# A gated linear-attention kernel with a low-rank mixer: six PSUM banks become one tile, read two or more banks at a time

## The chip, the cores and the metric

The kernel runs on one core of a Trainium2 chip. The core has TensorE (matrix products; PE for the products, PEld for the weight loads in the profile), VectorE (DVE), ScalarE (ACT), GpSimd (POOL) and SyncE (SP, which here only issues transfers). TensorE writes its results into PSUM, which has eight banks of 512 fp32 values in each of 128 partitions; VectorE and ScalarE read them there. The metric is the device time of one launch in microseconds (us), lower is better; a time is the median of several runs. Everything is fp32.

## What is computed

Two blocks follow each other. The first is a recurrence over 768 positions for 4 batches and 8 heads of 48 values, with a complex gate for each position and channel; the second mixes its result over positions with a rank-32 product and over channels with a two-layer network.

```python
scale = np.minimum(mag, 0.999) / (mag + 1e-06)      # mag = |a_re + i a_im|
a_re_n, a_im_n = (a_re * scale, a_im * scale)
for t in range(S):
    new_re = ar * S_re - ai * S_im
    new_im = ar * S_im + ai * S_re
    kv = np.einsum('bhd,bhe->bhde', k[:, :, t], v[:, :, t])
    S_re, S_im = (new_re + kv, new_im)
    y[:, :, t] = np.einsum('bhd,bhde->bhe', q[:, :, t], S_re)
...
h = x.transpose(0, 2, 1) @ U @ V                    # x: (4, 768, 384), from y
u = x + h.transpose(0, 2, 1)
return u + np.maximum(u @ w_ch1, 0.0) @ w_ch2       # w_ch1: 384 x 1536
```

## The kernel before

The 24 pieces of 128 positions (6 for each batch) are called chunks, and each is cut into two halves of 64 positions. For a chunk the gates are turned into logarithms and phases and summed over the positions by products with a triangular matrix (L744, L748 and L808 to L814), and become factors `es`, `cs`. `prep` multiplies q and k by them (L459) into `qkc`, turns each of q and k by 16 small transposes into two PSUM banks, one for each half (L869), and ScalarE copies each bank to `QK` (L875). `chain` then makes the products inside the halves (L898, masked into `AT` by VectorE, L901), the state of each half (L918; VectorE adds it to the running state `GM` and `G` through the helper `bounded`, L465), and the output of the chunk in two banks `y`: first `inside` (L948), AT times v, then `before` (L956), q times the state that went in, first for half 0 and then for half 1, accumulated onto it. ScalarE copies the two banks to `xo` (L965, L967).

`mixer` works on pairs of chunks (12 pairs, `m`). It makes the rank sums (L991), spreads them back over four banks (L1014) which VectorE adds to `xo` one bank at a time (`mixed`, L1019), turns `xo` into two banks (L1033) which VectorE and ScalarE copy to `uT`, one each (L1038), and then makes the two layers: `up` (L1052) for the first pairs and `up_fewer` (L1159), a scheme with fewer products whose sums are collected in `h` by ScalarE (L1167) and VectorE (L462, L1171), for the others; then `down` (L1248) and `down_two` (L1291), whose sums VectorE adds to `xo` before the transfer out (L1235).

Six of the eight PSUM banks are shared by all of this: six tiles `BANKS[0..5]` of 128 x 512, handed round in turn to every result that is not `up`, `down`, or (for most pairs) two of the five sums of `up_fewer`. Those use two banks of their own (`psM`), in which the results are called `up`, `down`, `few` and so on in the profile; what lies in the six is called `bank`. Waits between engines are not written by hand: the framework follows, tile by tile, what each instruction reads and writes and sets semaphores from it.

The order of work on every engine is written out: each helper (`PE`, `ACT`, `DVE`, `POOL`, `SP`) records an operation (a group of instructions) in `plan`, and at the end `plan.order()` emits them in the sequence of the list `ORDER`, 2190 numbers long. On each engine the instructions keep that order. `SPARE` puts some products of the identity ahead of early operations (`idle`, L1441 and L1445); their results are not used.

## Time and profile before

| | us |
|---|---|
| median of 3 runs | 540.3 (540.25 to 540.9) |
| the profiled execution | 539.81 |
| its span (first to last instruction) | 537.9 |
| TensorE products busy | 514.1 |
| TensorE weight loads busy | 468.5 |
| VectorE busy | 421.6 |
| ScalarE busy | 294.8 |
| mean granted TensorE clock | 0.995 of full |

A row of instruction groups names the line, the engine, the operation, output<-inputs, the shapes and the count; then the group's busy time, the mean duration of one in ns, and the idle time of its engine just before it, with what ended that. In a timeline the two leading numbers are the start and the length in us. A row of a table by stage has the stretch, its length, and for each engine its busy time and number of instructions, then the granted clock, the share of the DMA engines and GB/s. Products are pipelined, so that the end of one is modelled and consecutive ones overlap: the pitch of a group, from its start to the start of the next, is its cost on TensorE.

### The profile page before, as it was taken

The page shows a single profiled execution, that of the slowest core. Times are in us where ns is not written, and L with a number is a line of the kernel's source. Part 1 is how long each engine was busy: PE and PEld are TensorE (multiplying, and loading weights), DVE is VectorE, ACT ScalarE, POOL GpSimd, SP SyncE. Part 2 cuts the span into 40 slices and gives each one's busy share as a digit, 9 for nine tenths or more (in the row PEclk, how much of TensorE's full clock was granted, in tenths as well). Part 3 has the DMA queues.
Part 4 walks back from the last instruction along what each step waited for, and adds up shares of the span by engine and source line. Part 5 has one row for each costly group of instructions (what it writes and reads, how often), then busy time and mean ns, then how long its engine had stood idle before and what let it go on. Part 6 is the DMA issues. An engine that isn't in the chain of part 4 may idle for free.

```text
span 537.9 us, 17099 instructions
## 1 busy us (share of the span) xinstructions
PE 514.1 (96%) x7482; PEld 468.5 (87%) x7482; DVE 421.6 (78%) x837; ACT 294.8 (55%) x528; POOL 31.8 (6%) x61
## 2 busy tenths in 40 slices
PE   2789999899999999999999999999999999999996
PEld 1677786757999999999999999999999999999996
DVE  8788988999999998797997797797788364746352
ACT  5879998884786876456746746444544412011100
POOL 1000000000020000100200000100010000000010
PEclk9989999999999999999999999999999999999999
DMA  9948987642337142412450620500141000000011
GB/s 225 193 85 202 196 147 192 199 67 46 61 91 128 31 84 46 87 41 46 87 110 24 108 44 14 109 1 16 18 96 41 4 9 16 9 16 1 1 46 34
DMA packets 150689, 39.94 MB, mean 74 GB/s; under 512 B 145912, under 2 KB 147408, under 8 KB 150608
## 3 DMA queue, kind: packets, MB, share of 16 engines
q1 hardware_dynamic: 148400, 34.43, 32.7%
q0 software_dynamic: 2208, 4.35, 2.4%
q8 instruction: 60, 0.98, 0.8%
q14 instruction: 21, 0.17, 0.1%
HBM read 33.60 MB, written 4.76 MB: 71 GB/s over the span
## 4 chain that ended last, share of the span: by engine, by line
PE 81%; DVE 8%; ACT 7%; DMA 2%; issue 1%; SPq 0%; DVEq 0%; ACTq 0%
PE down L1291 29%; PE few L1159 13%; PE bank L1159 12%; PE bank L898 4%; PE bank L869 4%; PE bank L956 3%; PE bank L918 3%; PE bank L948 2%; PE up L1052 2%; PE bank L1014 1%; PE bank L808 1%; ACT gate L456 1%; DMA stage<-in_moe_w_ch_dram 1%; ACT cs L456 1%; PE bank L744 1%
## 5 line engine op out<-in xcount | busy, mean ns | idle before, releaser
L1291 PE MATMUL down<-w,h 128*128 128x192 f32 x396 | 73.1, 331 | 0.0
L875 ACT COPY QK<-bank 112x512 f32<-112x512 f32 x96 | 51.9, 593 | 26.3 <-PE bank L869 24.5
L1291 PEld LDWEIGHTS down<-w,h 128*128 128x128 f32 x396 | 64.3, 190 | 1.4
L462 DVE TENSOR_TENSOR xo<-down,xo 128x192 f32<-128x192 f32 (+1 forms) x79 | 30.1, 387 | 22.6 <-PE down L1291 22.3
L1167 ACT COPY h<-bank 128x512 f32<-128x512 f32 x25 | 14.3, 587 | 58.1 <-PE bank L1159 58.1
L456 ACT ACTIVATE gate<-gate 128x768 f32<-128x768 f32 (+1 forms) x50 | 39.8, 797 | 9.7 <-DVE wide L716 5.9
L459 DVE TENSOR_TENSOR QKC<-qk,cs 128x768 f32<-128x768 f32 x48 | 44.9, 952 | 0.1
L1291 PE MATMUL down<-stage 128*128 128x192 f32 x198 | 37.5, 330 | 0.0
L1052 PE MATMUL up<-uT,w 128*128 128x256 f32 x144 | 34.2, 387 | 2.0 <-ACT h L456 0.9
L1167 ACT COPY h<-few 128x512 f32<-128x512 f32 x35 | 20.4, 588 | 23.4 <-PE few L1159 23.4
L1291 PEld LDWEIGHTS down<-stage 128*128 128x128 f32 x198 | 32.4, 190 | 0.7
L1052 PEld LDWEIGHTS up<-uT,w 128*128 128x128 f32 x144 | 26.4, 190 | 7.2 <-ACT extra L456 1.5
L462 DVE TENSOR_TENSOR h<-bank,h 128x512 f32<-128x512 f32 x16 | 11.0, 690 | 27.3 <-PE bank L1159 16.8
L453 ACT ACT_TABLE_LOAD x24 | 30.8, 1283 | 1.1 <-PEq L1497 0.7
L869 PE MATMUL bank<-ident,QKC 64*112 64x64 f32 x768 | 29.2, 222 | 1.7 <-DVE GM L929 1.3
L869 PEld LDWEIGHTS bank<-ident,QKC 64*112 64x112 f32 x768 | 24.5, 132 | 7.2 <-issue 2.0
L794 POOL DMA_DIRECT2D gate<-F x15 | 12.0, 798 | 317.4 <-DVE F L817 177.6
L1159 PE MATMUL bank<-extra,w 128*128 128x128 f32 x232 | 30.1, 276 | 0.1
L1235 POOL DMA_DIRECT2D out_dram<-xo x32 | 19.7, 683 | 166.6 <-DVE xo L462 126.7
L1159 PEld LDWEIGHTS bank<-extra,w 128*128 128x128 f32 x232 | 28.2, 192 | 0.4 <-DVE AT L901 0.3
L456 ACT ACTIVATE cs<-F 128x384 f32<-128x384 f32 x48 | 23.8, 518 | 8.3 <-DVE F L817 7.1
L456 ACT ACTIVATE es<-bank 128x384 f32<-128x384 f32 x48 | 20.2, 497 | 14.6 <-PE bank L744 13.5
(185 smaller groups left out, 1179.0 us busy)
## 6 DMA issues: line engine op xcount, KB each, us to landing
stage<-in_moe_w_ch_dram SPq DMA_DIRECT2D x12, 768.0 KB
gate<-in_a_re_dram SPq DMA_DIRECT2D x24, 192.0 KB
gate<-in_a_im_dram SPq DMA_DIRECT2D x24, 192.0 KB
qk<-in_q_dram SPq DMA_DIRECT2D x24, 192.0 KB
qk<-in_k_dram SPq DMA_DIRECT2D x24, 192.0 KB
VP<-in_v_dram SPq DMA_DIRECT2D x24, 192.0 KB
out_dram<-xo POOLq DMA_DIRECT2D x12, 192.0 KB, 2.5
out_dram<-xo POOLq DMA_DIRECT2D x20, 96.0 KB, 2.4
```

What stands on the lines that cost most here:

```text
L453: ACT(1.4, rank, lambda: nc.scalar.preload_act_table_set(name), writes=[TABLE])
L456: return nc.scalar.activation(out=o, in_=i, func=f, **kw)
L459: nc.vector.tensor_tensor(out=o, in0=a, in1=b, op=OP.mult)
L462: nc.vector.tensor_tensor(out=o, in0=a, in1=b, op=OP.add)
L869: nc.tensor.transpose(out=get(*ps[r])[0:DQ, h], in_=get(*qkc)[at, h].rearrange("p u d -> p (u d)")[:, 0:DQ], identity=ident[at, at], tile_ ...
L875: nc.scalar.copy(out=get(*QK)[:, u].rearrange("p (h t) -> p h t", t=CH)[:, :, r * HC:(r + 1) * HC], in_=get(*ps[r])[0:DQ])
L898: nc.tensor.matmul(out=get(*ps0)[r:r + HC, h], lhsT=k_of(h, r, HC), rhs=q_of(h, r, HC), start=True, stop=True, tile_position=(0, r))
L1052: nc.tensor.matmul(out=get(*ps)[:, e], lhsT=w1[:, f, (ff + e) * 128:(ff + e + 1) * 128], rhs=get(*uT)[:, f], start=(f == 0), stop=(f == KD ...
L1159: nc.tensor.matmul(out=get(*ps)[:, q], lhsT=w()[:, q * 128:(q + 1) * 128], rhs=v[0](), start=(n == 0 and q == 0), stop=True, skip_group_ch ...
L1167: ACT(c_act(n3 * CH) - 0.045, RU, lambda i=i, k=k: nc.scalar.copy(out=at(i, k), in_=get(*ps)), [ps], [o])
L1235: queue.dma_start(out=out[b, c * CH:(c + 1) * CH, lo:hi], in_=get("xo", i)[:, lo:hi])
L1291: nc.tensor.matmul(out=get(*to)[:, part], lhsT=x(j), rhs=y[:, j], start=(first and j == 0), stop=(j == KH - 1), skip_group_check=not first)
```

## The change

The six bank tiles become one tile `BANKS` of 128 x 6 x 512; `bank_of` notes which bank a result has, and `beside` merges results that lie in neighbouring banks into one access. With it:

- `prep`: ScalarE copies both halves of a turned q or k by one instruction where the two banks are neighbours (40 of 48), by two where they are bank 5 and bank 0.
- `mixed`: VectorE adds the spread sums of up to four banks by one instruction: 19 instructions for 48.
- `turned`: for most pairs ScalarE alone copies both banks to `uT` (one instruction of 768 elements for each partition, or two of 384), where VectorE and ScalarE copied one each. VectorE has 9 copies fewer, ScalarE 2 more.
- `chain`: `before` (both halves) is recorded ahead of `inside`, and starts the accumulation; `inside` no longer names the states among what it reads.
- `ORDER` is another list, of 2097 numbers; one entry of `SPARE` moves with the numbering.

TensorE has the same 4233 matrix instructions. The number of neighbouring groups on TensorE with a different shape of its array (whole, halves of rows, halves of columns, quarters and so on) goes from 209 to 199. ScalarE's copies go from 245 to 207; VectorE's additions and multiplications of two tensors go from 497 to 468.

```diff
 SPARE = {
-    122: 2, 132: 10, 193: 14, 217: 5,
+    122: 2, 132: 10, 193: 14, 215: 5,
 }
...
@@ -378,9 +374,11 @@
     plan = Plan()
     makers, T, pools = {}, {}, {}
     banks = pool("banks", space=PSUM)
-    BANKS = [banks.tile([128, 512], FP, name="bank%d" % n) for n in range(6)]
-    for a in BANKS:
-        nc.vector.memset(a[HC // 2:HC], 0.0)
+    NB = 6
+    BANKS = banks.tile([128, NB, 512], FP, name="banks")
+    for n in range(NB):
+        nc.vector.memset(BANKS[HC // 2:HC, n], 0.0)
+    bank_of = {}
 
     def buffer(base, tag, bufs, shape, space=None, padded=None):
 
@@ -405,14 +403,25 @@
         if tag == "M":
             buffer(base, "psM", 2, shape, PSUM, padded)
             return
-        plan.buffer(base, "psS", len(BANKS), True)
+        plan.buffer(base, "psS", NB, True)
 
         def view():
-            a = BANKS[sum(plan.tag.get(b) == "psS" for b in T) % len(BANKS)]
+            bank_of[base] = sum(plan.tag.get(b) == "psS" for b in T) % NB
+            a = BANKS[:, bank_of[base]]
             size = padded or shape
             a = a[0:shape[0], 0:math.prod(size[1:])]
             return a[:, 0:shape[1]] if len(shape) == 2 else a.rearrange("p (x y) -> p x y", x=size[1])[:, 0:shape[1], 0:shape[2]]
         makers[base] = view
+
+    def beside(ps):
+
+        out = []
+        for n in range(len(ps)):
+            if n and bank_of[ps[n]] == bank_of[ps[n - 1]] + 1:
+                out[-1][1] = n + 1
+            else:
+                out.append([n, n + 1])
+        return [(lo, hi, BANKS[:, bank_of[ps[lo]]:bank_of[ps[lo]] + hi - lo]) for lo, hi in out]
 
 
     def c_act(n):
@@ -870,10 +879,11 @@
                                             identity=ident[at, at], tile_position=(r * HC, 0))
             PE(TURN, R1, turn, [qkc], ps, takes=[QK], way=5, steps=2 * H)
 
-            for r in range(2):
-                def keep(u=u, r=r, ps=ps):
-                    nc.scalar.copy(out=get(*QK)[:, u].rearrange("p (h t) -> p h t", t=CH)[:, :, r * HC:(r + 1) * HC], in_=get(*ps[r])[0:DQ])
-                ACT(c_act(HH * CH) - 0.06, R1, keep, [ps[r]], [QK + ((u, r),)])
+            def keep(u=u, ps=ps):
+                to = get(*QK)[:, u].rearrange("p (h r t) -> p r h t", r=2, t=HC)
+                for lo, hi, a in beside(ps):
+                    nc.scalar.copy(out=to[:, lo:hi], in_=a[0:DQ].rearrange("p r (h t) -> p r h t", t=HC))
+            ACT(c_act(2 * HH * CH) - 0.06, R1, keep, ps, [QK + (u,)])
 
 
 
@@ -946,7 +956,7 @@
                     for u in range(2):
                         h, at = 2 * p + u, slice(r * HC, (r + 1) * HC)
                         nc.tensor.matmul(out=get(*y[u])[side(r, u), p], lhsT=get(*ATi)[at, h], rhs=get(*VPi)[at, h],
-                                         start=(p == 0), stop=(c == 0 and r == 0), tile_position=(r * HC, (r ^ u) * HC),
+                                         start=(c == 0 and r == 0 and p == 0), stop=True, tile_position=(r * HC, (r ^ u) * HC),
                                          skip_group_check=True)
 
         def before(r):
@@ -954,12 +964,13 @@
                 for u in range(2):
                     h = 2 * p + u
                     nc.tensor.matmul(out=get(*y[u])[side(r, u), p], lhsT=q_of(h, r * HC, HC),
-                                     rhs=get(*(mid_G if r else ("G", i - 1)))[:, h], start=False, stop=True,
+                                     rhs=get(*(mid_G if r else ("G", i - 1)))[:, h], start=(p == 0), stop=False,
                                      tile_position=(0, (r ^ u) * HC), skip_group_check=True)
-        PE(0.44, RR, inside, [VPi, ATi, mid_G] + ([("G", i - 1)] if c else []), y, way=3, takes=[xi], steps=4 * H)
         if c:
             PE(0.467, RR, lambda: before(0), [QK, ("G", i - 1)], [y[0] + (0,), y[1] + (0,)], way=1, steps=2 * H)
         PE(0.467, RR, lambda: before(1), [QK, mid_G], [y[0] + (1,), y[1] + (1,)], way=1, steps=2 * H)
+        PE(0.44, RR, inside, [VPi, ATi], y, way=3, takes=[xi], steps=4 * H)
+
         def halves(a):
             return a.rearrange("p (a u d) -> p a u d", u=2, d=D)
         ACT(c_act(HH * D) + 0.02, RR, lambda: nc.scalar.copy(out=halves(get(*xi))[:, :, 0], in_=get(*y[0])), [y[0]], [xi + (0,)])
@@ -1016,31 +1027,41 @@
             PE(0.45, R0, products, [r, ("V", 0)] + [uT + ("kept",)] * (m >= AHEAD), ps, way=4, steps=4 * NP)
             return ps
 
-        def mixed(n, ps):
-            u = XO[i0 // MC % len(XO)].rearrange("p c (f n t) -> p n c f t", n=NP, t=R)[:, n]
-            DVE(c_dve(MC * RC), R0, lambda: add(u, get(*ps)[:, 0:MC].rearrange("p c (f t) -> p c f t", t=R), u), [ps],
-                [("xo", i0 + cc) for cc in range(MC)])
+        def mixed(ps):
+            u = XO[i0 // MC % len(XO)].rearrange("p c (f n t) -> p (c f) n t", n=NP, t=R)
+
+            def f():
+                for lo, hi, a in beside(ps):
+                    add(u[:, :, lo:hi], a[:, :, 0:MC * RC].rearrange("p n (f t) -> p f n t", t=R), u[:, :, lo:hi])
+            DVE(c_dve(MC * DM) + 0.1, R0, f, ps, [("xo", i0 + cc) for cc in range(MC)])
 
         def turned():
             us = [("xo", i0 + cc) for cc in range(MC)]
             tr = [out_of("uTp", ("pair", m, r), [128, MC * KD, HC], [128, H, HC]) for r in range(2)]
+            late = plan.tag[tr[0]] != "psS"
 
             def turn():
                 for cc in range(MC):
                     for f in range(KD):
                         for r in range(2):
                             at = slice(r * HC, (r + 1) * HC)
-                            nc.tensor.transpose(out=get(*tr[r])[:, cc * KD + f], in_=get(*us[cc])[at, f * 128:(f + 1) * 128],
+                            nc.tensor.transpose(out=get(*tr[r])[:, f * MC + cc], in_=get(*us[cc])[at, f * 128:(f + 1) * 128],
                                                 identity=ident[at, at], tile_position=(r * HC, 0))
             PE(0.39, R0, turn, us, tr, way=5, steps=2 * KD * MC)
-            for r in range(2):
-                def keep(copy, r=r):
-                    copy(out=get(*uT).rearrange("p f (c s t) -> p s c f t", c=MC, t=HC)[:, r],
-                         in_=get(*tr[r]).rearrange("p (c f) t -> p c f t", c=MC))
-                if r:
-                    ACT(c_act(MC * KD * HC) - 0.045, R0, lambda keep=keep: keep(nc.scalar.copy), [tr[r]], [uT + (r,)])
-                else:
-                    DVE(c_dve(MC * KD * HC), R0, lambda keep=keep: keep(nc.vector.tensor_copy), [tr[r]], [uT + (r,)])
+            def keep(copy, lo, hi, a):
+                copy(out=get(*uT).rearrange("p f (c s t) -> p (f c) s t", c=MC, t=HC)[:, :, lo:hi],
+                     in_=a[:, :, 0:MC * KD * HC].rearrange("p s (f t) -> p f s t", t=HC))
+
+            def both():
+                for x in beside(tr):
+                    keep(nc.scalar.copy, *x)
+            if ahead or late:
+                for r, (add_to, c, copy) in enumerate(((DVE, c_dve(MC * KD * HC), nc.vector.tensor_copy),
+                                                       (ACT, c_act(MC * KD * HC) - 0.045, nc.scalar.copy))):
+                    add_to(c, R0, lambda r=r, copy=copy: copy(
+                        out=get(*uT).rearrange("p f (c s t) -> p (f c) s t", c=MC, t=HC)[:, :, r], in_=get(*tr[r])), [tr[r]], [uT + (r,)])
+            else:
+                ACT(c_act(2 * MC * KD * HC) - 0.045, R0, both, tr, [uT + (0,)])
 
         def up(ff):
             ps = out_of("up", (m, ff), [128, 2, N], None)
@@ -1341,8 +1362,7 @@
                 ranked()
             for ff in range(0, NP, 2):
                 corrected(ff)
-        for n, ps in enumerate(spread()):
-            mixed(n, ps)
+        mixed(spread())
         if m >= AHEAD:
             turned()
         if m < AHEAD:
```

## Prediction

> **What bounds the kernel now.** I read the page first, then the table by stage, then who waited for whom.

> ```profile
> span 537.9 us, 17099 instructions
> ...
> PE 514.1 (96%) x7482; PEld 468.5 (87%) x7482; DVE 421.6 (78%) x837; ACT 294.8 (55%) x528; POOL 31.8 (6%) x61
> ...
> PE 81%; DVE 8%; ACT 7%; DMA 2%; issue 1%; SPq 0%; DVEq 0%; ACTq 0%
> ```
> ```profile
> 10.20:33.00 22.80, 17.91 (x248) 14.51 (x248) 19.26 (x33) 18.31 (x32) 0.00 (x0) 0.95 0.92 193
> 33.00:60.00 27.00, 26.66 (x456) 20.07 (x456) 23.61 (x41) 23.61 (x45) 0.00 (x0) 0.98 0.70 156
> 60.00:97.00 37.00, 35.82 (x737) 27.66 (x734) 32.04 (x57) 34.30 (x60) 0.95 (x1) 1.00 0.80 174
> 97.00:127.40 30.40, 28.14 (x123) 18.20 (x121) 28.49 (x46) 23.48 (x35) 1.52 (x2) 1.00 0.46 101
> 127.40:200.00 72.60, 72.48 (x1402) 67.23 (x1402) 69.85 (x130) 51.56 (x92) 5.24 (x8) 1.00 0.44 82
> 200.00:300.00 100.00, 100.00 (x1411) 95.47 (x1411) 83.81 (x172) 60.79 (x111) 9.25 (x14) 1.00 0.32 61
> ```
> ```profile
> PE bank L748 <- DVE GL L462: 10.2, 1, 10.2
> PE bank L918 <- ACT QK L875: 1.7, 1, 1.7
> ```

> From 127.4 us on TensorE is never idle; its stream of products alone sets the time. Ahead of that it is idle for 10.2 us at the start and then for 4.9 + 0.3 + 1.2 + 2.3 = 8.7 us (first column after the length against the length, first four rows). So the change can win little by faster copies: there is hardly a wait to take away. What it can lose is the overlap that keeps TensorE full, and that can be seen in one place:

> ```profile
> 391.44 1.11 PE L869 MATMUL bank<-ident,QKC 64*112 64x64 f32 x32
> ...
> 391.94 0.95 DVE L459 TENSOR_TENSOR QKC<-qk,cs 128x768 f32<-128x768 f32 x1
> 392.15 2.05 ACT L875 COPY QK<-bank 112x512 f32<-112x512 f32 x4 [0.93 <-PE bank L869]
> 392.48 0.81 PEld L918 LDWEIGHTS bank<-VP,QKC 64*48 64x48 f32 x64
> 392.48 0.94 PE L918 MATMUL bank<-VP,QKC 64*48 64x48 f32 x64
> ```

> ScalarE reads four turned banks from 392.15 to 394.20, and meanwhile TensorE writes the states into two others (392.48). Six tiles make this possible.

> **The change: one tile.** Waits come from what the framework notes for each tile. In both built programs I followed the wait values of the semaphores: for each access of TensorE, VectorE or ScalarE to one of the six banks, are the other engines' last accesses to any of the six, earlier in the program, known to be over? Before, in 3,011 of 7,608 such pairs; after, in all 7,457. One tile is treated as one thing: a product into bank 5 waits for the copy out of banks 3 and 4, and a ScalarE copy waits for a VectorE read of another bank. A typical pair of rows of the two programs:

> ```
> before: L1038 TensorCopy uT<-bank_65 128x2x3x64 [waits PE_49]
> after:  L1052 TensorCopy uT<-banks 128x768 [waits DVE_49,PE_49]
> ```

> So all work on the six banks is one chain through three engines, in the order of the program. Only TensorE's work on the two other banks (`down`, `up`, part of `few`) still runs beside reads, where it stands between them in the order. I price that gap by gap: a gap is a run of reads between two stretches of products into the six banks. The changed program has 184 gaps with 410 reads: 241 by ScalarE, 169 by VectorE. Their rows:

> ```profile
> L875 ACT COPY QK<-bank 112x512 f32<-112x512 f32 x96 | 51.9, 593 | 26.3 <-PE bank L869 24.5 <-DVE QKC L459 1.8
> L456 ACT ACTIVATE gate<-gate 128x768 f32<-128x768 f32 x43 | 36.2, 843 | 9.5 <-DVE wide L716 5.8 <-DMA gate<-in_a_im_dram 3.0
> ...
> L456 ACT ACTIVATE es<-bank 128x384 f32<-128x384 f32 x48 | 20.2, 497 | 14.6 <-PE bank L744 13.5 <-PE bank L748 1.0
> L967 ACT COPY xo<-bank 64x192 f32<-64x192 f32 x48 | 15.0, 314 | 11.7 <-PE bank L956 11.0
> ...
> L1167 ACT COPY h<-bank 128x512 f32<-128x512 f32 x25 | 14.3, 587 | 58.1 <-PE bank L1159 58.1
> L456 ACT ACTIVATE F<-bank,magic 128x384 f32<-128x384 f32 x24 | 13.9, 580 | 15.7 <-PE bank L808 14.7 <-PE bank L811 0.6 <-PE bank L814 0.3
> ...
> L1038 ACT COPY uT<-bank 128x384 f32<-128x384 f32 x10 | 4.8, 478 | 18.2 <-PE bank L1033 18.2
> ```
> ```profile
> L1171 DVE CUSTOM_DVE_ANT_1 h<-bank,h 128x512 f32<-128x512 f32 x32 | 21.6, 687 | 8.2 <-ACT h L1167 4.6 <-PE bank L1159 3.2
> L901 DVE COPY_PREDICATED AT<-mask,bank 128x512 f32<-128x512 int32 x24 | 17.6, 732 | 8.5 <-ACT xo L967 4.6 <-PE bank L898 3.6
> L462 DVE TENSOR_TENSOR xo<-bank,xo 128x192 f32<-128x192 f32 x48 | 15.3, 352 | 5.6 <-PE bank L1014 5.5
> L817 DVE SCALAR_TENSOR_TENSOR F<-F,bank 128x384 f32<-128x384 f32 x24 | 13.2, 549 | 6.7 <-ACT F L456 6.6
> ...
> L465 DVE CUSTOM_DVE_ANT_0 GM<-bank,G 112x384 f32<-112x384 f32 x20 | 11.1, 555 | 2.3 <-PE bank L918 1.5 <-ACT extra L456 0.2
> ...
> L462 DVE TENSOR_TENSOR h<-bank,h 128x512 f32<-128x512 f32 x16 | 11.0, 690 | 27.3 <-PE bank L1159 16.8 <-ACT h L1167 10.5
> ```

> The merged forms aren't in the trace. The 112x1024 copy costs at least what 768 elements cost (0.84 us) and at most two copies of 512 (1.19); the line through 0.314 (192) and 0.593 (512) gives 0.15 + 0.00087 n, so 1.03 us, near the middle, which I take (over 40 copies the bounds are 6 to 8 us apart from it). The merged sums lie on VectorE's line, 0.15 + 0.00105 n, between 0.35 and 0.95 us, and cannot cost more than the additions they replace.

> ScalarE: 40 x 1.03 + 16 x 0.593 + 48 x 0.497 + 24 x 0.58 + 25 x 0.587 + 72 x 0.315 (L965 as L967) + 7 x 0.82 + 5 x 0.478 + 1.2 for four small ones = 135 us. VectorE: 44 x 0.555 (GM, G) + 24 x 0.732 + 24 x 0.549 + 32 x 0.687 + 16 x 0.69 + 12.5 for the 19 merged sums (6 x 0.352 + 2 x 0.555 + 6 x 0.755 + 5 x 0.955) + 5 for ten others = 106 us. Together 241 us.

> Each gap also has its handing over, which these rows show:

> ```profile
> 452.32 1.06 PE L1159 MATMUL bank<-uT,gate 128*128 128x128 f32 x8
> ...
> 453.22 1.14 PE L1291 MATMUL down<-w,stage 128*128 128x192 f32 x6
> 453.42 0.69 DVE L1171 CUSTOM_DVE_ANT_1 h<-bank,h 128x512 f32<-128x512 f32 x1
> ```
> ```profile
> 98.75 0.59 ACT L456 ACTIVATE extra<-up 128x512 f32<-128x512 f32 x1
> ...
> 99.39 2.46 PEld L1052 LDWEIGHTS up<-uT,w 128*128 128x128 f32 x12 [1.24 <-ACT extra L456]
> ...
> 103.44 0.84 ACT L456 ACTIVATE gate<-gate 128x768 f32<-128x768 f32 x1
> ...
> 104.32 0.96 DVE L720 SCALAR_TENSOR_TENSOR GL<-gate,GL 128x768 f32<-128x768 f32 x1 [0.18 <-ACT gate L456]
> ```

> TensorE to reader 0.20 us (453.42 after its stream ended at 453.22), reader to TensorE 0.05 (99.34 to 99.39), reader to reader 0.04 (104.28 to 104.32). 184 x 0.25 + 65 changes of reader x 0.04 = 49 us. All gaps: 241 + 49 = 290 us.

> **What hides it.** From each gap I take TensorE's own work on the two other banks that stands in it, by pitches: 6 products of L1291 0.97 us (below), 8 of L1159 0.90 (452.32 to 453.22), and so on; what it has more than the gap is lost. Example: after a chunk's transposes (L869) come GM, the merged copy of q, G and two copies of k: 0.555 + 1.03 + 0.555 + 2 x 0.593 = 3.33, with handing over 3.70 us; two groups of L1291 stand there, 1.95 us; TensorE is idle for 1.75. Where nothing stands there, as between the products of one chunk's halves (L898) and the next step, the 0.73 of L901 is idle with its 0.25. Over the 184 gaps 136 us are hidden, 55 gaps wholly, and 154 us are not: 54 up to the last product of L1248 (127.4 us before), 100 behind it.

> **The rest.**
> ```profile
> 186.68 0.97 PE down L1291 x6
> ...
> 188.51 1.17 PE down L1291 x6
> ```
> A group beside one of another array shape costs some 0.1 us more at each end (1.17 against 0.97); 10 changes of shape fewer at about 0.15 us are -1.5 us. The idle 8.7 us of the first stages take up as much of the first 54. `before` ahead of `inside` has the same products and waits for GM and G as before; I give it nothing, since GM's and G's time is in the gaps. ScalarE alone copying `uT` is in the gaps as well; without them it would be 0.82 us for two at a time of 0.55. The order of loads on SP moves a little; transfers land ahead of need from 127.4 us on (DMA share 0.44 and less), and a slower TensorE only eases that.

> **Sum.** The profiled execution is 539.8 us (span 537.9 and 1.9 around it; the median of the runs is 540.3). 539.8 - 1.5 + 154 - 8.7 = 684 us.

> [...] The granted clock is 0.95 in the stage with 4.9 us of idle TensorE (10.2:33), 0.98 and 1.00 behind it. [...]

> **Rivals.**
> 1. *The waits are hollow, and the change does what it means to.* If reads were always over before TensorE comes to its next group, only -1.5 us and up to 3.8 us of idle time from 33 us on (0.34 + 1.18 + 2.26) remain: 535 to 538, say 537, faster. For it: in the old program reads of one bank are indeed over when it comes round again. Against it: a bank came round only after five other results; now the wait is for the newest read. It decides if uncovered gaps together fall below 10 us, against 154.
> 2. *Serial, but gentler.* Handing over costs nothing in addition (reads start while the stream drains): 121 us uncovered, of which 8.7 absorbed: 539.8 - 1.5 + 121 - 8.7 = 651.
> 3. *VectorE's and ScalarE's other work gets into the chain.* They work in order, so a multiplication of `QKC` (0.95) ahead of a read delays it where TensorE's work since that engine's last read is shorter. Counted so, 180 us are uncovered, nothing is absorbed: 718; with the clock at 0.95 throughout, another 0.05 x 514 = 26: 744.
> 4. *Reads come much earlier than their place*, half of the gaps vanish: 540 + 70 = 610.

> **Chances.** The forecast with rival 2 (640 to 710) 0.68; rival 3 (710 to 770) 0.20; rival 4 (545 to 640) 0.08; rival 1 0.03; no change 0.01. Predicted 684 us; range 635 to 755. Faster by over 0.2% (about what a measurement of this kernel can tell from no change) 0.03, within 0.2% 0.01, slower 0.96.

> **What would show it.** TensorE's busy share falls from 96% to about 75% at the same 4233 instructions; in 200:300 its busy time is 70 to 80 of 100 us instead of 100. Among the waits stand `PE banks` <- `ACT QK` and `PE banks` <- `DVE` with tens of us each, TensorE waiting for reads of banks that it isn't about to write, and `ACT QK` <- `DVE G`, read behind read. The merged copy shows about 1.03 us. The groups of L1291, between themselves, keep 0.97. I am wrong if TensorE is still full in 200:300, or if its idle time is put down to loads or to a lower clock.

## The result and the profile after

| | before | after |
|---|---|---|
| median of the runs, us | 540.6 (540.25 to 541.59, 4 runs) | 767.95 (767.06 to 771.3, 4 runs) |
| span of the profiled execution, us | 537.9 | 765.9 |
| mean granted TensorE clock | 0.995 | 0.901 |

The change makes the kernel slower by a factor of 1.421 (95% interval 1.417 to 1.426). In three of the experiments below (two tiles, three tiles unmerged, 176 added products) one run of four lies over 1.5% above the fastest; the medians include it, the ratios and intervals leave it out. The page of the changed kernel shows it at once: TensorE has the same 7482 records and is busy for a smaller share, the third row (the granted clock in 40 slices) has fives and a six in the first fifth, and in the chain that ended last VectorE and ScalarE now hold 32%, which was 15%.

```profile
span 765.9 us, 16997 instructions
...
PE 589.6 (77%) x7482; PEld 514.7 (67%) x7482; DVE 417.3 (54%) x799; ACT 298.2 (39%) x490; POOL 32.9 (4%) x61
...
PEclk9856958589998987999999998998999999999999
...
PE 62%; DVE 17%; ACT 15%; issue 4%; DMA 0%; DVEq 0%; ACTq 0%
```

The table by stage of the changed kernel (busy time of TensorE is the first column after the length; the granted clock is the third number from the end). Where the old kernel had 26.66 of 27 us, 35.82 of 37 and 100 of 100 us busy, this one has 17.19, 23.99 and 75.24:

```profile
33.00:60.00 27.00, 17.19 (x254) 13.62 (x254) 11.38 (x23) 10.23 (x13) 0.00 (x0) 0.53 0.37 78
60.00:97.00 37.00, 23.99 (x266) 15.80 (x264) 18.26 (x29) 18.58 (x31) 0.00 (x0) 0.78 0.35 72
97.00:150.00 53.00, 38.51 (x656) 28.85 (x654) 22.12 (x34) 24.57 (x43) 0.00 (x0) 0.66 0.49 102
...
200.00:300.00 100.00, 75.24 (x1134) 66.36 (x1132) 63.15 (x112) 44.80 (x75) 5.29 (x8) 0.90 0.28 54
```

The clock column is the surprise: 0.53 from 33 to 60 us, where the kernel before had 0.98. To TensorE's one long wait at the start (L757, 10.6 us; before, L748, 10.2) come many for other engines' reads: its records leave 139 idle places of over 20 ns, 81 of them of 0.8 to 3 us. The waits (engine and line, what ended the wait: us in total, times, longest):

```profile
PE banks L928 <- ACT QK L885: 16.4, 10, 3.3
PE banks L1180 <- DVE h L1192: 11.8, 8, 2.2
PE banks L757 <- DVE GL L471: 10.6, 1, 10.6
PE banks L1180 <- ACT h L1188: 10.4, 15, 1.9
...
PE banks L966 <- DVE AT L911: 7.9, 5, 3.4
...
PE banks L878 <- ACT xo L976: 3.7, 3, 2.2
```

One place in the timeline of the changed kernel (start, length) answers to the place at 391 us that the prediction shows. By the program the states (L928) are written into banks 2 and 3, the turned q or k is read from banks 4 and 5, and `uT` from banks 0 and 1:

```profile
565.47 1.01 ACT L885 COPY QK<-banks 112x1024 f32<-112x1024 f32 x1 [1.13 <-PE banks L1048]
...
566.53 0.57 PE L928 MATMUL banks<-VP,QKC 64*48 64x48 f32 x32 [1.11 <-ACT QK L885]
567.17 0.80 ACT L1052 COPY uT<-banks 128x768 f32<-128x768 f32 x1 [0.69 <-PE banks L928]
...
568.03 0.57 PE L928 MATMUL banks<-VP,QKC 64*48 64x48 f32 x32 [0.92 <-ACT uT L1052]
```

TensorE starts 0.05 us after ScalarE's copy of `QK` has ended (566.48), stops after half of the states, because a copy of `uT` stands next in the program's order, and goes on 0.06 us after that has ended. None of the three touches a bank of another. Before, the same products ran while ScalarE read.

### The profile page after: what moved, and what is told of

The parts are those of the page before. It is cut to its first block, busy times and chain, and to the rows that moved or that the text cites. A ratio compares the mean times of both kernels' runs of the same rounds, so it can differ in the third digit from the quotient of the medians.

```text
span 765.9 us, 16997 instructions
## 1 busy us (share of the span) xinstructions
PE 589.6 (77%) x7482; PEld 514.7 (67%) x7482; DVE 417.3 (54%) x799; ACT 298.2 (39%) x490; POOL 32.9 (4%) x61
## 4 chain that ended last, share of the span: by engine, by line
PE 62%; DVE 17%; ACT 15%; issue 4%; DMA 0%; DVEq 0%; ACTq 0%
PE down L1312 17%; PE banks L1180 10%; PE few L1180 8%; ACT QK L885 4%; PE banks L908 4%; PE banks L966 4%; PE banks L878 3%; PE up L1073 3%; PE banks L928 3%; DVE h L1192 3%; PE banks L958 2%; ACT h L1188 2%; DVE AT L911 2%; ACT es L465 2%; ACT gate L465 2%
## 5 line engine op out<-in xcount | busy, mean ns | idle before, releaser
L885 ACT COPY QK<-banks 112x1024 f32<-112x1024 f32 (+1 forms) x56 | 48.6, 891 | 83.1 <-PE banks L878 16.7
L1312 PE MATMUL down<-w,h 128*128 128x192 f32 x396 | 79.5, 350 | 0.9 <-DVE h L1192 0.9
L1312 PEld LDWEIGHTS down<-w,h 128*128 128x128 f32 x396 | 71.3, 206 | 2.5 <-DVE h L1192 1.5
L1188 ACT COPY h<-banks 128x512 f32<-128x512 f32 x25 | 14.3, 587 | 94.9 <-PE banks L1180 84.9
L878 PE MATMUL banks<-ident,QKC 64*112 64x64 f32 x768 | 32.4, 232 | 18.2 <-ACT xo L976 3.7
L465 ACT ACTIVATE gate<-gate 128x768 f32<-128x768 f32 (+1 forms) x50 | 39.7, 796 | 13.0 <-DVE wide L725 9.6
L928 PE MATMUL banks<-VP,QKC 64*48 64x48 f32 x1408 | 27.1, 223 | 22.9 <-ACT QK L885 16.4
L878 PEld LDWEIGHTS banks<-ident,QKC 64*112 64x112 f32 x768 | 26.5, 139 | 25.2 <-ACT xo L976 4.2
L908 PE MATMUL banks<-QK 112*64 112x64 f32 x768 | 32.4, 249 | 12.6 <-DVE F L826 4.1
L928 PEld LDWEIGHTS banks<-VP,QKC 64*48 64x48 f32 x1408 | 23.3, 136 | 27.2 <-ACT QK L885 17.9
L1180 PE MATMUL banks<-extra,w 128*128 128x128 f32 x232 | 33.6, 292 | 10.3 <-ACT h L1188 4.8
L911 DVE COPY_PREDICATED AT<-mask,banks 128x512 f32<-128x512 int32 x24 | 17.4, 725 | 42.6 <-PE banks L966 15.7
L1312 PE MATMUL down<-stage 128*128 128x192 f32 x198 | 39.7, 341 | 0.3 <-DVE xo L471 0.3
L908 PEld LDWEIGHTS banks<-QK 112*64 112x64 f32 x768 | 29.3, 161 | 15.2 <-DVE F L826 4.5
L1180 PEld LDWEIGHTS banks<-extra,w 128*128 128x128 f32 x232 | 30.1, 203 | 12.5 <-ACT h L1188 6.0
L1192 DVE CUSTOM_DVE_ANT_1 h<-banks,h 128x512 f32<-128x512 f32 x32 | 21.5, 688 | 25.3 <-PE banks L1180 19.2
L1312 PEld LDWEIGHTS down<-stage 128*128 128x128 f32 x198 | 33.8, 197 | 1.3 <-DVE xo L471 0.6
```

Source lines behind the costliest of these rows:

```text
L465: return nc.scalar.activation(out=o, in_=i, func=f, **kw)
L878: nc.tensor.transpose(out=get(*ps[r])[0:DQ, h], in_=get(*qkc)[at, h].rearrange("p u d -> p (u d)")[:, 0:DQ], identity=ident[at, at], tile_ ...
L885: nc.scalar.copy(out=to[:, lo:hi], in_=a[0:DQ].rearrange("p r (h t) -> p r h t", t=HC))
L908: nc.tensor.matmul(out=get(*ps0)[r:r + HC, h], lhsT=k_of(h, r, HC), rhs=q_of(h, r, HC), start=True, stop=True, tile_position=(0, r))
L911: DVE(0.17 + 0.00104 * H * HC, RL, lambda: nc.vector.copy_predicated(out=get(*ATi), mask=mask.bitcast(I32).unsqueeze(1).to_broadcast([128, ...
L928: nc.tensor.matmul(out=get(*dk[r])[x:x + D, h], lhsT=get(*ks)[at, h, x // DP, 0:D], rhs=get(*VPi)[at, h], start=True, stop=True, tile_posi ...
```

## The experiments

### Six tiles again, all else as after

```diff
-    BANKS = banks.tile([128, NB, 512], FP, name="banks")
+    PER = 1
+    BANKS = [banks.tile([128, PER, 512], FP, name="bank%d" % n) for n in range(NB // PER)]
...
-            a = BANKS[:, bank_of[base]]
+            a = BANKS[bank_of[base] // PER][:, bank_of[base] % PER]
...
-            if n and bank_of[ps[n]] == bank_of[ps[n - 1]] + 1:
+            if n and bank_of[ps[n]] == bank_of[ps[n - 1]] + 1 and bank_of[ps[n]] % PER:
```

> The changed kernel with its six banks as six tiles again; an access of several banks becomes one for each bank; the new order, the states' products first and ScalarE's copies of uT stay. Theory (the one tile makes all work on the banks one chain): 535 to 552 us, TensorE busy 95% or more, granted clock 0.99 or more, no wait of a product for a read of another bank. Rival (the new order or the states-first sums cost the time, the tile little): 650 us or more, with TensorE idle as in the changed kernel.

Measured: 538.18 us (ratio 0.9959, interval 0.9948 to 0.9971), and in a second series 537.79. Page and waits of this kernel:

```profile
span 535.5 us, 17117 instructions
...
PE 513.9 (96%) x7482; PEld 468.4 (87%) x7482; DVE 414.7 (77%) x828; ACT 298.0 (56%) x537; POOL 32.4 (6%) x61
```
```profile
PE bank L758 <- DVE GL L472: 10.2, 1, 10.2
PE bank L929 <- ACT QK L886: 1.3, 1, 1.3
PE bank L879 <- DVE GM L940: 1.0, 1, 1.0
```

The whole loss is gone, and TensorE waits for nearly nothing. The new order, the states' products ahead of the products inside a chunk, and ScalarE's copies of `uT` together make the kernel 2.4 us faster than before, not slower. So neither the order nor `before` ahead of `inside` makes the change slow.

### One tile, all else as before

```diff
-    BANKS = [banks.tile([128, 512], FP, name="bank%d" % n) for n in range(6)]
+    ALL = banks.tile([128, 6, 512], FP, name="banks")
+    BANKS = [ALL[:, n] for n in range(6)]
```

> The kernel before with its six bank tiles made one tile and nothing else: old order, nothing merged. Theory: slower than before by more than 140 us (the gaps of the old order by the same reckoning are 141 us uncovered without any handing over, 232 us with it), so 680 to 830 us, granted clock 0.93 or less, every bank access ordered behind the last of the other engines. Rival (the order or the merged instructions are the cause): 540 to 560 us.

Measured: 788.10 us (1.4587, 1.4538 to 1.4635), clock 0.885. Two lines that leave every product and every read as it was cost 247.5 us, in the upper part of the range expected of the one tile alone; the order of after and its merged accesses are not needed for the loss. The page:

```profile
span 786.8 us, 17107 instructions
...
PE 603.6 (77%) x7482; PEld 527.6 (67%) x7482; DVE 424.6 (54%) x837; ACT 297.3 (38%) x528; POOL 32.2 (4%) x61
```

### Tiles of two and of three banks

The same edit as in the first experiment with `PER = 2` and `PER = 3`.

> The changed kernel with three tiles of two banks each; results are merged only where both lie in one tile. Theory (what serializes is the tile): a read holds back two banks and not six, so most gaps have other bank work to stand in them: 560 to 650 us, granted clock between 0.90 and 1.00. Rival (the wider instructions themselves are what is slow): 700 us or more, as they are nearly all kept.

> The changed kernel with two tiles of three banks each; results are merged only where both lie in one tile. Theory (the loss follows the number of banks that one read holds back): between three tiles (618 us) and one tile (768 us), 660 to 720 us, granted clock between 0.92 and 0.97. Rival (one tile is special, with two tiles one is always free): 640 us or less.

Measured: three tiles 618.13 us (1.1449, 1.1418 to 1.148), clock 0.971; two tiles 676.79 us (1.25, 1.2392 to 1.2608), clock 0.942. With six tiles, three, two and one the time is 538, 618, 677 and 768 us. The stretch from 200 to 300 us, for six, three and two tiles in this order:

```profile
200.00:300.00 100.00, 100.00 (x1451) 95.54 (x1449) 81.01 (x168) 62.13 (x111) 9.33 (x14) 1.00 0.33 64
```
```profile
200.00:300.00 100.00, 93.53 (x1450) 88.12 (x1447) 77.36 (x150) 59.26 (x105) 6.55 (x10) 0.98 0.31 55
```
```profile
200.00:300.00 100.00, 85.35 (x1454) 77.37 (x1453) 70.81 (x135) 53.60 (x92) 6.16 (x9) 0.95 0.33 62
```

Both lie in the ranges of the theory. The programs show why, by the count that the prediction makes (pairs of accesses by two engines of which the earlier is known to be over): 3,126 of 7,608 with six tiles, 4,850 of 7,515 with three, 6,086 of 7,489 with two and all 7,457 with one. The more banks one read holds back here, the emptier TensorE (100, 93.5, 85.4 and, with one tile, 75.2 us busy in this stretch) and the lower the clock in it (1.00, 0.98, 0.95 and 0.90); one tile is no special case.

### What merging is worth

Nothing is merged: once with the one tile, once with three tiles of two banks.

```diff
-            if n and bank_of[ps[n]] == bank_of[ps[n - 1]] + 1:
+            if False:
```

> The changed kernel with its one tile and its order, but nothing merged: one access for each bank. Theory: 40 copies of 1.01 us become two of 0.59 each (+7 us), the sums 29 more additions (+4 us of fixed cost), 70 more steps of the chain at 0.04 (+3 us), a part of it covered: 772 to 785 us. Rival (merged reads are themselves what is slow): under 760 us.

> As three (three tiles of two banks), but nothing merged: one access for each bank. Theory (merged access is worth a fixed part of an instruction wherever the chain is uncovered): 22 to 24 merged copies and sums become two each, up to 31 more accesses at 0.15 to 0.2 us, so 620 to 626 us. Rival (merging costs, since a wider read holds its banks longer): 612 us or less.

Measured: with one tile 781.81 us (1.4471, 1.4435 to 1.4508), as the theory had it; with three tiles 620.03 (1.1391, 1.1307 to 1.1474), which can't be told from the 618.13 with merging; the 2 to 8 us that the theory had there are not decided. The row of the copy in the changed kernel, beside that of the kernel before (in the prediction, 593 ns for 512), explains about half of the 13.9 us:

```profile
L885 ACT COPY QK<-banks 112x1024 f32<-112x1024 f32 x40 | 40.2, 1012 | 68.0 <-PE banks L878 12.4 <-DVE G L474 11.4 <-PE banks L757 9.2
```

1.01 us for two copies' 1.19, 7 us over 40 copies. The merged forms do what they are for, as far as one tile leaves the reads uncovered; what they are worth with separate tiles isn't shown. The change now falls into three parts, since the kernel with one tile and nothing merged differs from the one with six tiles only in the tile: order and the rest -2.4 us (540.6 to 538.2), the one tile +243.6 (538.2 to 781.8), merging -13.9 (781.81 to 767.95).

### Is the lower clock a part of the loss?

Products of the identity are added into the next free one of the two other banks, where the plan's costs leave a gap of the chain uncovered; their results are not used. In the second kernel the fraction is 0.8, the constant 0.2 and the divisor 0.224; in the third, besides, they stand only ahead of the first result of `up`.

```diff
     for at, n in enumerate(seq):
...
+        bank = any(plan.tag[b] == "psS" for b in plan.ops[n][6])
...
+                reps = int(0.7 * (run + 0.25 - cover) / 0.125) if run else 0
...
+                    for _ in range(reps):
+                        idle_into(ms[nxt])
```

> The changed kernel with 311 or fewer added products of the identity (128x128, about 0.12 us each at full clock, 39 us in all) into the free one of the two other banks, put where a gap of the chain is not covered; their results are not used. Theory (some 50 us of the loss are a lower granted clock, which comes with TensorE's many short stalls): the clock rises from 0.90 to 0.95 or more and the time falls to 710 to 750 us although work is added. Rival (the clock has another cause, or costs nothing since it falls on waits): clock 0.90 as before, 766 to 800 us.

> As fill, but with 176 added products, sized by the pitch that fill showed (two records of 0.112 us each, 0.224 us for a product, 39 us in all) to stay inside the gaps they stand in. In the changed kernel TensorE's busy time at half clock is 119 us, so 55 to 60 us of its loss are the clock's. Theory (the clock's share is real time): the time at half clock falls from 151 us to 100 us or less, and the time to 740 to 757 us. Rival (the clock falls only on stalls, so that its loss costs nothing): 764 us or more whatever the clock does.

> As fill2, but only the 56 products (12.5 us) that stand ahead of the first result of up (72.9 us in the changed kernel); behind it nothing is added. In the changed kernel TensorE is at half clock from 34.4 to 71.9 us, 25 us of it busy. Theory (a window of 3.41 us under about half busy halves the clock, and only a window at least 85% busy brings it back, so short stalls keep it low): full clock up to 72 us, and the time 8 to 11 us below the changed kernel's 768 (757 to 760). Rival (the clock's loss falls on stalls): 765 us or more with the clock at full there as well.

Measured: 764.23 us (1.4098 to 1.4198) at clock 0.953; 762.79 (1.3998 to 1.4211) at 0.943; 763.31 (1.4093 to 1.4161) at 0.919. The clock rose as expected each time, but the time fell by only 3.7 to 5.2 us: neither theory's numbers came, and for all but the third the interval touches that of the changed kernel. I had mis-sized the first: a product is two records, 0.224 us, so 311 of them are 70 us, while the idle time between TensorE's records fell by only 48 us (160.7 to 112.4). In the second, 39.4 us of products replaced 34.6 us of idle time (160.7 to 126.1). What these added products gave back in clock they mostly took again.

At the one place where the half clock lasts longest and the other banks are free, the gain can be seen by itself. The stages of the changed kernel, in which the clock is half from 34.4 to 71.9 us, are above. Here is one of its groups of transposes, then the same group in the third kernel with added products, and that kernel's stages:

```profile
81.84 0.66 PE L878 MATMUL banks<-ident,QKC 64*112 64x64 f32 x16
```
```profile
74.09 1.10 PE L878 MATMUL banks<-ident,QKC 64*112 64x64 f32 x16
```
```profile
33.00:60.00 27.00, 21.98 (x378) 18.61 (x378) 13.01 (x25) 12.45 (x20) 0.00 (x0) 1.00 0.49 111
60.00:97.00 37.00, 25.82 (x372) 19.45 (x370) 18.82 (x30) 19.28 (x30) 0.00 (x0) 0.80 0.36 77
97.00:150.00 53.00, 38.81 (x522) 27.96 (x522) 22.34 (x35) 25.84 (x44) 0.00 (x0) 0.63 0.43 87
```

The group is reached 7.75 us earlier although 12.5 us of products were added. So the half clock was on the path there. Of it 4.9 us are left when the products of `down` begin (L1269; 177.8 for 182.7 us), and 3.9 at the end of the span: the clock falls in other places instead (at half for 3.4 us from 71.7 and from 119.5 us on, where the changed kernel has nothing like it, and for 6.8 us from 170.7 us on, where that has 3.4).

### Nine products ahead of the one stretch at half clock

A last test on the six tiles, where nothing else stalls: this kernel has one stretch at half clock, from 27.2 to 34.1 us. Two rows of its table by stage, the 3.44 us ahead of that stretch and its first 3.40 us:

```profile
23.76:27.20 3.44, 1.82 (x84) 1.53 (x84) 3.34 (x5) 3.40 (x6) 0.00 (x0) 1.00 1.03 315
27.20:30.60 3.40, 2.05 (x44) 1.71 (x44) 3.23 (x7) 1.77 (x3) 0.00 (x0) 0.51 0.91 168
```

The 3.44 us ahead of it were 53% busy, and their longest idle time 1.3 us. The edit adds nine products in the two gaps, 5 ahead of one group of states and 4 ahead of one of transposes:

```diff
+        for _ in range({223: 5, 218: 4}.get(n, 0)):
+            idle_into(into)
```

> six with 9 added products (2 us) in the two gaps ahead of its one stretch at half clock: that of 1.32 us at 25.5 us and those of 1.00 and 0.34 us at 28 us. The stretch is 6.8 us with 5.5 us busy. Theory of the busy share: the window ahead of it (0.54 busy) comes above 0.7, no stretch at half clock, and up to 2.7 us saved where the products fit in the gaps: 535.5 to 537.5 us, under six_again by 0.5 to 2.5. Rival (that stretch is hidden behind reads or loads, or the products push what follows): 538 us or more.

> The kernel of six once more, beside six_fill on the same chip: 537 to 539 us, 0.3 to 0.6% under the kernel before.

Measured: 535.78 us (0.9914, 0.9897 to 0.9931) against 537.79 (0.9951, 0.9936 to 0.9967) for the same kernel without them. Added work makes it 2.0 us faster, and TensorE has no half clock left until its last product (the records have it only from 531.4 us on, with no product in it); the three rows here are 94%, 87% and 90% busy, at a clock of 1.00:

```profile
22.85:26.26 3.41, 3.20 (x106) 2.77 (x105) 3.31 (x5) 3.35 (x5) 0.00 (x0) 1.00 1.02 310
26.26:29.68 3.42, 2.96 (x48) 2.29 (x47) 3.25 (x6) 2.95 (x6) 0.00 (x0) 1.00 0.77 154
29.68:33.09 3.41, 3.08 (x75) 2.78 (x77) 3.27 (x8) 2.20 (x4) 0.00 (x0) 1.00 0.47 91
```

This is the fastest version of the study, 4.7 us under the kernel before: six tiles, the new order, nothing merged, and nine products that nobody reads.

## Why the direction was right and the size was not

The sum was 684 us, the range 635 to 755, the median is 768. To see which term failed I set the changed kernel's trace against that of the six tiles. Both have the same products in the same order, so that 7480 of 7482 records could be paired; each pair's distance to the next was compared. Together the distances grew by 229.8 us (the spans differ by 230.4): 179.7 at 139 places where TensorE was idle for over 20 ns ahead of the next record, 44.7 where it was not idle but at half clock, and 5.3 elsewhere (1.9 of them ahead of 20.7 us, where the clock is not on record; see the last section). The idle time between records, 160.7 us in all, was then divided by what went on meanwhile: 123.0 while ScalarE or VectorE accessed a bank, 15.6 while one of them did other work that stands ahead of its next bank access (13 to 20, by how strictly "ahead" is taken), 22.1 in neither. The kernel of six tiles is itself idle for 3.3 us at these places, so another 22.3 us (179.7 + 3.3 - 160.7) are stalls that the records hide, as a product's modelled end lies behind its stream: in the prediction's rows at 452 us by 0.16 us (453.38 for 453.22), and 139 times that is 22.

| term | predicted, us | measured, us |
|---|---|---|
| reads of banks not covered | 121 (rival 2) | 123.0 |
| handing over | 33 (154 - 121) | 44 (22.1 + 22.3), by exclusion |
| other work of ScalarE and VectorE ahead of a read | 0 | 15.6 |
| old idle time absorbed | -8.7 | -3.3 |
| lower clock | 0 | 44.7 |
| order, shape changes | -1.5 | -2.4 |
| elsewhere | 0 | 5.3 |
| sum | 144 | 227 |

- **What bounds the kernel, and that the change can lose its overlap.** Right: with the overlap back (six tiles) TensorE is at 96% again. But the clock went with it, which the prediction did not count.
- **One tile makes one chain.** Right, and shown from both sides: taken away, the loss goes; put alone into the kernel before, it comes. The added waits are the program's: the kernel with six tiles uses the same six banks without them, in 538.2 us.
- **The reads.** 121 us forecast, 123.0 measured, and 129 gaps not wholly hidden (184 - 55) for 139 stalls. Only the sums are compared, so that some of the closeness may be luck: up to the last product of L1248 the distances at idle places grew by 58 us, for 45 forecast (54 less 8.7), and behind it by 122, for 100. The merged copy, estimated at 1.03 us, takes 1.012.
- **The handing over** was 11 us short if what is left over is all of that kind, which isn't shown; and of the 8.7 us that I took off for old idle time only 3.3 were there.
- **Rival 3** named both things that failed: other work in the chain, for which it had 26 us more (180 for 154; 15.6 measured), and the clock, for which it had another 26 at 0.95. It ended at 744, and its range of 710 to 770, which has the measured 768, had a chance of 0.20.
- **The step that failed is the clock.** The prediction shows 0.95 in the stage with 4.9 us of idle TensorE, but its sum has no term for a lower clock. No run shows that the sum could stay without one: the changed kernel is at 0.901. It has 18 stretches at half clock (the last at its very end), 151 us together with 119 us of them busy. The 3.41 us ahead of each of the other 17 were 10% to 63% busy, and their longest idle time was 1.1 to 3.1 us; neither of the two longest idle gaps behind the start (3.64 and 3.71 us, as counted) begins such a stretch (the first lies within one). The clock was put at nothing and cost 44.7 us of the 84 by which the sum was short; the rest is the other work (15.6), the handing over (11), old idle time (5) and small differences. The added products show that it lies on the path in the first stretch (7.75 us), while how much of the rest would come back at full clock couldn't be tried without adding work.
- **What would show it.** Busy share 77% (about 75% said), 75.24 in 200:300 (70 to 80 said), the waits of `banks` on `ACT QK` and `DVE` (16.4 and 11.8 us for the largest rows; over all of TensorE's lines 31.7 for `ACT QK`, and 19, 16 and 13 for VectorE's `h`, `F` and `AT`), and read behind read: 11.4 us in the row of the merged copy are put down to `DVE G`. The group of L1291, now L1312, keeps its pitch at full clock: 571.53, 572.50, 573.48 in this timeline, 0.97 and 0.98 us.

```profile
571.53 1.14 PE L1312 MATMUL down<-stage,h 128*128 128x192 f32 x6
...
572.50 1.14 PE L1312 MATMUL down<-stage 128*128 128x192 f32 x6
...
573.48 1.14 PE L1312 MATMUL down<-stage,h 128*128 128x192 f32 x6
```

What would have proved me wrong, idle time put down to loads or to a lower clock, did not come: the waits name reads. But the sign was aimed the wrong way round: where added products lowered the idle time from 160.7 to 112.4 us, the clock rose from 0.901 to 0.953, so here the clock followed the idle time, and the loss is both.

## What to carry to other kernels

A tile is the unit of waiting: before buffers that turn round between engines are joined into one tile, count what is written and read at the same time, for a merged access saves a tenth of a microsecond or two and the join can cost the whole overlap (13.9 us against 243.6 here). If joining is wanted, join only what is always read together. And the chain of short stalls had two prices here: the stalls (179.7 us), and the half clock of what ran between them (44.7 us), so that a few unused products in a gap paid for themselves where TensorE sets the end (2.0 us for nine), but hardly where the chain does (3.7 to 5.2 us of 768 for 56 to 311).

## What the runs showed of the clock

The granted clock in the records of the kernel before and of the changed one is 1 or 0.5. Of their 20 stretches at 0.5 (2 and 18) the last of each runs into the end; the other 18 are 3.41 us long or 2, 6, 8 or 11 times that. The records begin late, at 13.65 and 20.73 us: in the changed kernel the products of the identity (L1461) ahead of the first record follow each other at 0.21 us and those behind it at 0.11, and within a recorded half clock, from 39.6 us on, such products (L1465) follow each other at 0.21. So a clock of 1.00 ahead of the first record, and the means of 0.995 and 0.901, leave out a stretch that runs like half clock.

```profile
30.97:34.38 3.41, 0.47 (x16) 0.33 (x12) 2.32 (x5) 1.01 (x1) 0.00 (x0) 1.00 0.68 127
34.38:37.79 3.41, 1.65 (x46) 1.49 (x48) 1.18 (x2) 1.75 (x2) 0.00 (x0) 0.50 0.12 24
...
68.50:71.93 3.43, 2.92 (x4) 1.17 (x4) 0.00 (x0) 1.25 (x4) 0.00 (x0) 0.50 0.00 0
```

Busy 14% of the first row, 48% of the second, 85% of the last. Eleven pieces in a row are at half clock, 37.5 us: the ten ahead of the last were 36% to 86% busy, with ten idle places of 0.63 to 3.40 us in the eleven, and the last holds four long records of the phases' products (L820 and L823, 68.74 to 71.67 us).
